# A causal-attention kernel with a channel mix behind it: the second batch's first pair of heads loaded ahead of the key weights, and the whole order of work written anew

## The chip, the cores and the metric

The kernel runs on one NeuronCore of a Trainium2 chip, as one program. The metric is the device time of one execution in microseconds (us), the median over runs. Engines are named as in the profile: PE is TensorE's matmuls and PEld its weight loads, DVE is VectorE, ACT is ScalarE, POOL is GpSimd and SP is SyncE. The DMA engines, 16 of them, move data for all.

## The reference

Inputs q, k and v have 8 batches of 8 heads, 576 rows and 64 columns, in float32. The first part is attention in which a row sees the blocks of 64 rows up to its own. Its output, with the heads side by side, is x of 8 x 576 x 512. The second part mixes each row with the one before it and sends it through three weight matrices.

```python
scores = scale * np.matmul(q, k.transpose(0, 1, 3, 2))
mask = block_i >= block_j            # blocks of 64 rows
attn = softmax(np.where(mask, scores, -1e9))
x = np.matmul(attn, v)               # heads side by side: B, S, 512
xk = mu_k * x + (1.0 - mu_k) * x_prev
xr = mu_r * x + (1.0 - mu_r) * x_prev
k = np.maximum(xk @ w_k, 0.0)
out = sigmoid(xr @ w_r) * (k * k @ w_v)
```

## The kernel before

The work is cut into 678 tasks. A task is one step of one engine, for example one load, one group of matmuls that fills a PSUM buffer, or one exponential. Each call of `add` (L67) makes one, and the functions below make them batch by batch. The order in which the tasks are written into the program is not that in which they are made: the table `ORDER` (L15) lists the tasks' numbers, each with a count of filler matmuls behind a plus sign, and `PLACE` (L53) names the engine of each task that may stand on several (P for POOL, D for DVE, A for ACT). `Plan.order` (L95) reads both. Each engine then does its own tasks strictly in that order, and waits where a task's inputs or its buffer are not ready. Buffers come from rings: four of PSUM (`ps`), four for q and k (`nb`), two each for their transposed forms (`qkt`), v as loaded (`lv`) and v in half precision (`vo`), ten for exponentials (`e`).

For each batch b the tasks are these, with the names that the text uses.

- Loads. `add_qk` (L235) loads k and q in pairs of heads on POOL's DMA queue (L249) and turns them on DVE (L260). For the first two batches (`HALVES`) a task loads two heads' rows with two DMAs, and the scores of a pair need only that pair. `add_v` (L272) loads v from SP (L284) and casts it (L207 to L216). `add_w` (L310) loads the key weights WK (four DMAs), the gate weights WR (two) and the value weights WV (four), all on POOL's queue (L324), after the first batch's q and k.
- Scores. `add_unit` (L349) multiplies k by q (L365) in small matmuls of 32 by 64 tiles, six units per batch, and takes the exponential on ACT (L386). For the first two batches a unit is cut into two halves of 8 to 24 matmuls, one per pair of heads. Later batches have units of 16 or 32 matmuls.
- Sums and products. `add_part` (L506, first batch, in two parts) and `add_av` (L426, the others) multiply the exponentials by a column picker for the sums (L524, L449) and by v (L544, L460: tasks T, A and B). DVE inverts the sums (L405 to L421) and normalises (L556, L489, L497) into `xt`.
- Mix. `add_mix` (L572) makes xk and xr of each quarter of the columns: a difference or two scalings on POOL, DVE or ACT (L580, L584), and two multiplications on DVE (L600, L604).
- Channel mix, for every 512 rows of all batches: `add_pk` (L623) is the key product (L644), its relu on ACT or DVE (L659, L661) and the square (L669, L671). `add_pr` (L677) is the gate product (L687) and a tanh (L697). `add_pv` (L703) is the value product (L721), the last multiplication on DVE (L731), and the store from SP (L740).

A first task, `spare` (L749), does 27 filler matmuls (L222) whose output nobody reads, until the first q and k are there. The other fillers stand ahead of sums and products: 1, 1 and 9 in the first batch.

Of the kernel before, what the change touches and what calls it, by code (L numbers as in the profile page):

```python
# [12 lines left out]
ALU = mybir.AluOpType  # L13

ORDER = """  # L15
# [35 lines left out]
"""  # L51

PLACE = (  # L53
    "DDDDPDPAPADDAPPAADAADPPDDPAPDPAAPPDADAPPPDAADAPDDAPDPDPDPAADPAAAADPAAA"
    "AAAAADPDADPAADPAPAPAPDDDAADAADPDAAPAAAPADAPADAADPADAA")


class Plan:
# [8 lines left out]
    def add(self, key, alts, fn, deps=(), uses=(), **info):  # L67
        t = {"key": key, "alts": alts, "eng": alts[0], "fn": fn,
             "deps": [d for d in deps if d is not None],
             "uses": list(uses), "fill": 0, "info": info}  # L70
        for b in t["uses"]:
            b["left"] += 1
        self.tasks.append(t)
        return t
# [37 lines left out]
def kernel(  # L112
# [12 lines left out]
    nc = tc.nc  # L125
    B, H, S, D = q.shape
    C = H * D
    DF = moe_w_k.shape[1]
    P = 128
# [3 lines left out]
    GH = 4  # L133
    QC = P // GH
    JT = S // D
    RW = 32
    TOK = S // RW
# [21 lines left out]
    LW = TOK * D  # L159
# [13 lines left out]
    def new(buf):  # L173

        return slots[buf["ring"], buf["slot"]]

    identb = consts.tile([P, P], BF)
# [21 lines left out]
    HALVES = (0, 1)  # L199
    add = plan.add  # L200
# [17 lines left out]
    def unread(t, dst):  # L218


        for _ in range(t["fill"]):
            nc.tensor.matmul(  # L222
                dst, identb,
                identb[:, :].unsqueeze(1).to_broadcast([P, 4, P]),
                start=True, stop=True)
# [9 lines left out]
    def add_qk(b, g, n):  # L235

        src, qkt = (q, k)[n], qkt_buf[b]
        nb = plan.buf("nb")  # L240

        def rows():
            return new(nb)

        def fetch(eng, me):
            parts = ([(D * y, D, GH * y + 2 * g, 2) for y in range(2)]
                     if b in HALVES else [(0, P, GH * g, GH)])
            for p0, np_, h0, nh in parts:
                nc.gpsimd.dma_start(  # L249
                    rows()[p0:p0 + np_],  # L250
                    src[b, h0:h0 + nh].rearrange(
                        "y (r j) d -> (y r) (j d)", j=TOK))
        t = add(f"qkld {b} {g} {n}", ("POOL",), fetch, uses=[nb], kind="ldc",
                kb=P * LW * 4 / 1024, starts=2 if b in HALVES else 1)

        if n:
            loads.setdefault(b, (nb, t))

        def turn(eng, me):
            nc.vector.transpose(  # L260
                new(qkt)[:, n, g].rearrange("p t e -> p (t e)").bitcast(
                    FP).rearrange("p (r j) -> p j r", r=RW),
                rows()[:, :].bitcast(FP).rearrange(
                    "p (j s) -> p j s", s=RW))
        evac["qkt", b, g, n] = add(f"turn {b} {g} {n}", ("DVE",), turn, [t],
                                   uses=[nb, qkt], kind="turn", cols=S)
# [436 lines left out]
    def add_pv(c, j0):  # L703
# [42 lines left out]

    wbuf = plan.buf("ps")

    add("spare", ("PE",), lambda eng, me: unread(me, new(wbuf)[:, 0]), uses=[wbuf],  # L749
        kind="spare", cols=[])  # L750
    mu_ready = []

# [81 lines left out]
```

## Time and profile before

| what | value |
|---|---|
| median of 3 runs | 260.37 us (259.85, 260.37, 262.7) |
| profiled execution | 262.33 us, of which the span from first to last instruction is 260.2 |
| mean granted TensorE clock | 0.980 |
| PE busy | 242.6 us, 93% of the span, 4058 matmuls |
| DVE, ACT, POOL busy | 188.8, 162.4 and 80.3 us |
| share of the chain that ended last | PE 84%, DMA 6%, ACT 3%, "issue" 3% |

Times in the profile count from the span's start. A busy PE is not PE at its peak, since a matmul's end is modelled. In the chain of work that ended last, a row gives a start, a duration and what ran or was waited for; the number behind an x is a count of instructions. "Issue" is time in which an engine waits for nothing that the program's own instructions tell. A row of busy time by stretches has, for each engine, the busy microseconds and the count of instructions that started, then the granted clock, the DMA engines' busy share and the GB/s that they moved. Idle time matters only on the engine that sets the end.

### The profile page before, as it was taken

The page shows a single profiled execution, that of the slowest core. Times are in us where ns is not written, and L with a number is a line of the kernel's source. Part 1 is how long each engine was busy: PE and PEld are TensorE (multiplying, and loading weights), DVE is VectorE, ACT ScalarE, POOL GpSimd, SP SyncE. Part 2 cuts the span into 40 slices and gives each one's busy share as a digit, 9 for nine tenths or more (in the row PEclk, how much of TensorE's full clock was granted, in tenths as well). Part 3 has the DMA queues.
Part 4 walks back from the last instruction along what each step waited for, and adds up shares of the span by engine and source line. Part 5 has one row for each costly group of instructions (what it writes and reads, how often), then busy time and mean ns, then how long its engine had stood idle before and what let it go on. Part 6 is the DMA issues. An engine that isn't in the chain of part 4 may idle for free.

```text
span 260.2 us, 8926 instructions
## 1 busy us (share of the span) xinstructions
PE 242.6 (93%) x4058; PEld 132.3 (51%) x4058; DVE 188.8 (73%) x233; ACT 162.4 (62%) x184; POOL 80.3 (31%) x88
## 2 busy tenths in 40 slices
PE   8859498879999999999999999999999999999994
PEld 3536356654454446644454487444554764444442
DVE  1737889597888699899688969884699389444322
ACT  1456048877656969796777786786887743274220
POOL 6074256841405610060455234420000221142000
PEclk9988989997999999999999999999999999999999
DMA  5999996899699995449785930021002200300224
GB/s 88 194 165 189 207 217 103 134 191 215 102 253 238 168 208 181 90 96 215 196 137 97 215 110 3 3 98 65 4 5 81 83 5 12 150 3 0 81 82 161
DMA packets 49189, 31.50 MB, mean 121 GB/s; under 512 B 38528, under 2 KB 39808, under 8 KB 49152
## 3 DMA queue, kind: packets, MB, share of 16 engines
q1 hardware_dynamic: 40128, 18.29, 29.7%
q0 software_dynamic: 6688, 12.06, 27.6%
q10 hardware_dynamic: 2336, 0.59, 1.5%
q8 instruction: 31, 0.51, 0.8%
q14 instruction: 6, 0.05, 0.1%
HBM read 33.56 MB, written 9.44 MB: 165 GB/s over the span
## 4 chain that ended last, share of the span: by engine, by line
PE 84%; DMA 6%; ACT 3%; issue 3%; DVE 1%; POOL 0%; ACTq 0%; DVEq 0%; POOLq 0%
PE t_ps L644 25%; PE t_ps L721 23%; PE t_ps L687 12%; PE t_ps L365 10%; PE t_ps L460 8%; PE t_ps L449 4%; DMA t_lv<-in_v_dram 4%; ACT t_e L386 2%; PE t_ps L544 2%; DMA t_nb<-in_k_dram 1%; DMA out_dram<-t_o 1%; PE t_ps L222 1%; DVE t_o L731 1%; PE t_ps L524 1%; ACT L293 0%
## 5 line engine op out<-in xcount | busy, mean ns | idle before, releaser
L386 ACT ACTIVATE t_e<-t_ps 128x1024 f16<-128x1024 f32 (+4 forms) x98 | 87.6, 957 | 30.9 <-PE t_ps L365 30.1
L644 PE MATMUL t_ps<-t_xk,WK 128*128 128x512 f16 (+3 forms) x416 | 66.9, 314 | 0.4 <-ACT t_e L386 0.3
L721 PE MATMUL t_ps<-WV,t_k 128*128 128x512 f16 (+1 forms) x296 | 64.6, 374 | 0.0
L671 POOL TENSOR_TENSOR t_k<-t_kr 128x1024 f16<-128x1024 f32 x16 | 30.5, 1907 | 76.9 <-DVE t_kr L661 62.5
L644 PEld LDWEIGHTS <-WK 128*128 128x128 f16 x416 | 37.0, 98 | 26.1 <-issue 2.4
L721 PEld LDWEIGHTS <-t_k 128*128 128x128 f16 x296 | 28.1, 98 | 33.1 <-issue 1.9
L365 PE MATMUL t_ps<-t_qkt 32*64 32x64 bf16 (+7 forms) x1344 | 37.3, 290 | 6.1 <-ACT t_e L386 3.8
L260 DVE STREAM_TRANSPOSE t_qkt<-t_nb 128x576 f32<-128x576 f32 x32 | 38.1, 1242 | 1.5 <-PE t_ps L365 1.0
L697 ACT ACTIVATE t_t<-t_ps 128x1024 f32<-128x1024 f32 x18 | 18.5, 1028 | 31.5 <-PE t_ps L687 31.5
L687 PE MATMUL t_ps<-WR,t_xr 128*128 128x512 f16 x144 | 35.1, 390 | 0.4 <-ACT t_e L386 0.4
L659 ACT ACTIVATE t_kr<-t_ps 128x1024 f32<-128x1024 f32 x22 | 22.4, 1024 | 18.8 <-PE t_ps L644 18.3
L365 PEld LDWEIGHTS <-t_qkt 32*64 32x64 bf16 x1344 | 21.8, 106 | 22.9 <-issue 17.9
L731 DVE SCALAR_TENSOR_TENSOR t_o<-t_t,t_ps 128x1024 f32<-128x1024 f32 (+2 forms) x20 | 22.1, 1108 | 14.9 <-PE t_ps L721 9.9
L661 DVE TENSOR_SCALAR t_kr<-t_ps 128x1024 f32<-128x1024 f32 x14 | 17.1, 1224 | 19.5 <-PE t_ps L644 19.4
L584 POOL TENSOR_TENSOR t_d<-t_xt 128x576 f32<-128x576 f32 (+2 forms) x10 | 11.6, 1162 | 36.3 <-DVE t_xk L604 13.5
L687 PEld LDWEIGHTS <-t_xr 128*128 128x128 f16 x144 | 13.7, 100 | 17.2 <-issue 2.5
L460 PE MATMUL t_ps<-t_e,t_vo 64*32 64x512 f16 (+7 forms) x1120 | 21.6, 295 | 0.0
L460 PEld LDWEIGHTS <-t_vo 64*32 64x32 f16 x1120 | 14.9, 95 | 8.8 <-issue 4.5
L604 DVE SCALAR_TENSOR_TENSOR t_xk<-t_d,MU,t_xt 128x576 f16<-128x576 f32 (+2 forms) x24 | 19.2, 802 | 0.1
L497 DVE TENSOR_TENSOR t_xt<-t_ps,t_rt 128x1024 f32<-128x1024 f32 x14 | 16.9, 1218 | 3.2 <-PE t_ps L460 3.1
L580 ACT ACTIVATE t_d<-t_xt,MU 128x576 f32<-128x576 f32 (+1 forms) x24 | 16.8, 751 | 3.7 <-DVE t_xr L604 2.6
L214 POOL CAST t_vo<-t_lv 128x1152 f16<-128x1152 f32 x8 | 9.7, 1216 | 30.5 <-PE t_ps L460 19.3
(40 smaller groups left out, 181.7 us busy)
## 6 DMA issues: line engine op xcount, KB each, us to landing
out_dram<-t_o SPq DMA_DIRECT2D x17, 512.0 KB, 3.3
t_lv<-in_v_dram SPq DMA_DIRECT2D x30, 288.0 KB, 6.3
t_nb<-in_k_dram POOLq DMA_DIRECT2D x12, 288.0 KB, 6.4
t_nb<-in_q_dram POOLq DMA_DIRECT2D x12, 288.0 KB, 6.2
t_nb<-in_k_dram POOLq DMA_DIRECT2D x8, 144.0 KB, 6.3
t_nb<-in_q_dram POOLq DMA_DIRECT2D x8, 144.0 KB, 6.3
WK<-in_moe_w_k_dram POOLq DMA_DIRECT2D x4, 256.0 KB, 6.7
WV<-in_moe_w_v_dram POOLq DMA_DIRECT2D x4, 256.0 KB, 9.0
```

Source lines behind the costliest of these rows:

```text
L260: nc.vector.transpose(new(qkt)[:, n, g].rearrange("p t e -> p (t e)").bitcast(FP).rearrange("p (r j) -> p j r", r=RW), rows()[:, :].bitcas ...
L365: nc.tensor.matmul(new(ms[a // 2])[y * D:y * D + D, a % 2, col:col + n], qkt[rows, 1, g, t * D:t * D + D, f], qkt[rows, 0, g, q0:q0 + n, f ...
L386: nc.scalar.activation(new(e)[:, 2 * h:2 * h + 2, 0:w], new(ms[h])[:, :, 0:w], AF.Exp, scale=ISQ)
L460: nc.tensor.matmul(PA[o, u, HALF + f * D:HALF + f * D + D] if kind == "T" else PA[o, u, lo - D:lo - D + n], weight(b, u, c, t % JT, f), E[ ...
L604: e.scalar_tensor_tensor(dst, dt[:, 0, 0:W], MU1[:, n, cc % 2, cc // 2:cc // 2 + 1], x, ALU.mult, ALU.add)
L644: nc.tensor.matmul(ps[:, x, y * w + a:y * w + a + n], WK[:, cc, jc * P:(jc + 1) * P], MIX[0][:, cc, at:at + n], start=(cc == 0), stop=(cc ...
L659: nc.scalar.activation(kt, ps, AF.Relu, scale=ROOT)
L671: (nc.vector if eng == "DVE" else nc.gpsimd).tensor_tensor(dst, KR, KR, ALU.mult)
L687: nc.tensor.matmul(ps[:, x], MIX[1][:, cc, g:g + P], WR[:, cc], start=(cc == 0), stop=(cc == CCn - 1))
L697: nc.scalar.activation(new(tb), new(m), AF.Tanh, scale=0.5)
L721: nc.tensor.matmul(ps[:, x, cols], k2[:, jc, at:at + P], WV[:, jc, cols], start=(jc == 0), stop=(jc == JCn - 1))
L731: nc.vector.scalar_tensor_tensor(new(o)[:, xs, cols], new(tb)[:, xs, cols], 1.0, new(m)[:, xs, cols], ALU.add, ALU.mult)
```

## The change

The two tables are written anew. Most of the 678 tasks stand in another place of the order, 71 of them on another engine; the last 21 stand as before. The two places below are those that the prediction speaks of. Numbers of buffers are part of the names: t_nb_107 to 110 are the four q and k buffers, t_ps_142 to 145 the four PSUM buffers, and t_e_115 to 124 the exponentials.

POOL, right behind the first batch's first value cast (a piece of the difference, - before, + now; the loads of 64 x 1152 are pairs of heads of the second batch):

```order
 L214 CAST t_vo_113<-t_lv_105 128x1152
-L324 DMA WK<-in_moe_w_k_dram 128x1024 x4
-L324 DMA WR<-in_moe_w_r_dram 128x1024 x2
 L249 DMA t_nb_107<-in_k_dram 64x1152 x2
-L584 ISA
-L584 TENSOR_TENSOR t_d_131<-t_xt_125 128x256
+L214 CAST t_vo_113<-t_lv_106 128x1152
 L249 DMA t_nb_108<-in_q_dram 64x1152 x2
+L328 DMA WK<-in_moe_w_k_dram 128x1024 x4
 L249 DMA t_nb_109<-in_k_dram 64x1152 x2
+L588 ISA
+L588 TENSOR_TENSOR t_d_131<-t_xt_125 128x256
```

The second batch's first k and q come ahead of WK, with a value cast between them that stood on DVE; the second pair follows WK, and WR, no longer in this piece, comes behind that pair.

ACT, from the end of the first batch's exponentials. Before (t_e_122 to 124 are the first three exponentials of the second batch; t_t_138 is the first gate product's tanh):

```order
L697 ACTIVATE t_t_138<-t_ps_143 128x1024
L580 ACTIVATE t_d_130<-t_xt_125,MU_157 128x320 x2
L386 ACTIVATE t_e_122<-t_ps_145 128x1024
L386 ACTIVATE t_e_123<-t_ps_144 128x1024
L386 ACTIVATE t_e_124<-t_ps_143 128x1024
L386 ACTIVATE t_e_115<-t_ps_145 128x1024
L386 ACTIVATE t_e_116<-t_ps_142 128x1024
L386 ACTIVATE t_e_117<-t_ps_143 128x2x320
```

And now (t_kr_132 and 133 are the relus of the first two key products, on DVE before):

```order
L390 ACTIVATE t_e_122<-t_ps_144 128x1024
L390 ACTIVATE t_e_123<-t_ps_142 128x1024
L390 ACTIVATE t_e_124<-t_ps_143 128x1024
L390 ACTIVATE t_e_115<-t_ps_144 128x1024
L390 ACTIVATE t_e_116<-t_ps_142 128x1024
L663 ACTIVATE t_kr_132<-t_ps_145 128x1024
L390 ACTIVATE t_e_122<-t_ps_143 128x1024
L663 ACTIVATE t_kr_133<-t_ps_144 128x1024
L390 ACTIVATE t_e_123<-t_ps_142 128x1024
L390 ACTIVATE t_e_124<-t_ps_145 128x1024
L701 ACTIVATE t_t_138<-t_ps_143 128x1024
```

The first five exponentials of the second batch now stand ahead of the first tanh, and the key products' relus stand among those of the second pair. PE's order is the same one: each exponential reads the PSUM buffer of the score step ahead of it, so five half score steps now come ahead of the first key product, and the gate product, which was the first step behind the first batch, comes after two key products and three more half steps.

The rest of the diff: the load of the first two batches is written with one loop over the halves and a source of three dimensions, with the same two DMAs; `spare` does its filler in two calls of 10 and 17 with an empty loop between them. The filler ahead of the first batch's second sums goes from 9 to 10, and the two single ones are gone.

```diff
 ORDER = """
-1 0+27 5 3 9 2 7 11 6 15 12 16 13 17 4 29 33 56 30 10 60 34 64 57 68 8 61 72
+1 5 0+27 3 9 7 2 11 15 12 6 16 13 17 4 29 33 56 30 10 60 34 64 57 68 8 61 72
...
 PLACE = (
-    "DDDDPDPAPADDAPPAADAADPPDDPAPDPAAPPDADAPPPDAADAPDDAPDPDPDPAADPAAAADPAAA"
+    "PADAPPDPDPPPDAAAPPPAAPPDPAAPDDDAPAPPDPDPPPDPAAADADAADADAADDADAAAPAAAPA"
...
         def fetch(eng, me):
-            parts = ([(D * y, D, GH * y + 2 * g, 2) for y in range(2)]
-                     if b in HALVES else [(0, P, GH * g, GH)])
-            for p0, np_, h0, nh in parts:
+            if b in HALVES:
+                for y in range(2):
+                    a = GH * y + 2 * g
+                    nc.gpsimd.dma_start(
+                        new(nb)[y * D:y * D + D, :],
+                        src[b, a:a + 2].rearrange(
+                            "h (r j) d -> h r (j d)", j=TOK))
+            else:
                 nc.gpsimd.dma_start(
-                    rows()[p0:p0 + np_],
-                    src[b, h0:h0 + nh].rearrange(
+                    rows(), src[b, GH * g:GH * g + GH].rearrange(
                         "y (r j) d -> (y r) (j d)", j=TOK))
...
-    add("spare", ("PE",), lambda eng, me: unread(me, new(wbuf)[:, 0]), uses=[wbuf],
+    SHORT = 0
+
+    def spare(eng, me):
+        dst, rest = new(wbuf)[:, 0], me["fill"]
+        me["fill"] = min(rest, 10)
+        unread(me, dst)
+        for n in range(SHORT):
+            at = n % GH * RW
+            nc.tensor.matmul(dst[at:at + RW, 0:D], identb[:, 0:RW],
+                             identb[:, 0:D], start=True, stop=True)
+        me["fill"] = max(rest - 10, 0)
+        unread(me, dst)
+    add("spare", ("PE",), spare, uses=[wbuf],
         kind="spare", cols=[])
```

More of the change, by code (lines that the diff above doesn't have):

```diff
@@ L15 @@
 ORDER = """
[35 rows of a table removed]
[35 rows of a table added]
 """
 PLACE = (
-    "DDDDPDPAPADDAPPAADAADPPDDPAPDPAAPPDADAPPPDAADAPDDAPDPDPDPAADPAAAADPAAA"
-    "AAAAADPDADPAADPAPAPAPDDDAADAADPDAAPAAAPADAPADAADPADAA")
+    "PADAPPDPDPPPDAAAPPPAAPPDPAAPDDDAPAPPDPDPPPDPAAADADAADADAADDADAAAPAAAPA"
+    "PAAAAAPADADAADDDPAAAPDPDPDAAAAADDAPAAADAPADDDAADPAADP")
 class Plan:
@@ L245, in fetch @@
         def fetch(eng, me):
-            parts = ([(D * y, D, GH * y + 2 * g, 2) for y in range(2)]
-                     if b in HALVES else [(0, P, GH * g, GH)])
-            for p0, np_, h0, nh in parts:
+            if b in HALVES:
[6 more added lines that the diff above has]
+            else:
                 nc.gpsimd.dma_start(
-                    rows()[p0:p0 + np_],
-                    src[b, h0:h0 + nh].rearrange(
+                    rows(), src[b, GH * g:GH * g + GH].rearrange(
                         "y (r j) d -> (y r) (j d)", j=TOK))
         t = add(f"qkld {b} {g} {n}", ("POOL",), fetch, uses=[nb], kind="ldc",
-                kb=P * LW * 4 / 1024, starts=2 if b in HALVES else 1)
+                kb=P * LW * 4 / 1024, starts=1 + (b in HALVES))
         if n:
```

68 rows, old and new, of the table ORDER are left out of this document.

## The prediction

> **What bounds the kernel now.** I read the page's slices first, then the chain that ended last in order of time, then busy time by stretches laid along what the chain showed. Slices are 6.5 us; the rows are TensorE's busy tenths, its granted clock and the DMA engines' share.
>
> ```profile
> PE   8859498879999999999999999999999999999994
> PEclk9988989997999999999999999999999999999999
> DMA  5999996899699995449785930021002200300224
> ```
>
> From the tenth slice (58.5 us) on TensorE is full until the last products. All loss that another order can win back lies in the first nine slices, where the DMA engines are full as well. The clock dips there three times. The chain names what TensorE waited for (start us, us, what):
>
> ```profile
> 16.94 0.77 DVE t_vo L214
> ...
> 18.23 0.41 issue
> ...
> 25.03 0.09 issue
> ...
> 27.52 3.79 issue
> 31.31 1.21 PE t_ps L544 x41
> 32.52 3.13 PE t_ps L687 x8
> 35.65 1.75 PE t_ps L644 x16
> 37.40 1.51 PE t_ps L365 x26
> ...
> 47.02 1.89 PE t_ps L687 x8
> ...
> 50.65 0.21 PE t_ps L460 x13
> 50.86 1.36 PE t_ps L449 x60
> ...
> 52.81 1.85 PE t_ps L644 x16
> 54.66 1.32 PE t_ps L460 x72
> ...
> 58.36 0.81 issue
> ...
> 62.74 3.56 PE t_ps L721 x16
> ...
> 66.31 0.59 PE t_ps L365 x31
> ...
> 73.81 1.40 PE t_ps L460 x79
> ```
>
> "Issue" is a wait for nothing that the program names, 3.79 us of it at one place. The gaps end at 18.64, 25.12, 31.31 and 59.17. Busy time between those ends (count of matmuls and of weight loads in brackets) and in the stretch ahead of them, and, in a fence of its own, in a later one with idle DMA engines:
>
> ```profile
> 11.10:18.63 7.53, 4.35 (x143) 2.77 (x132) 2.88 (x5) 5.69 (x9) 4.30 (x7) 0.96 1.12 167
> 18.63:25.11 6.48, 6.39 (x128) 3.81 (x128) 5.58 (x12) 4.16 (x5) 2.90 (x6) 0.78 1.14 197
> 25.11:31.30 6.19, 2.40 (x128) 1.87 (x128) 5.00 (x11) 0.00 (x0) 2.30 (x5) 1.00 1.13 206
> ...
> 53.40:59.16 5.76, 3.83 (x129) 2.53 (x127) 5.69 (x8) 4.86 (x6) 1.66 (x3) 0.99 1.19 193
> ```
>
> ```profile
> 155.45:159.19 3.74, 3.74 (x128) 2.64 (x133) 3.74 (x5) 2.65 (x4) 3.73 (x3) 1.00 0.02 4
> ```
>
> ```profile
> q8 instruction: 31, 0.51, 0.8%
> ```
>
> The stalls are 256 TensorE instructions apart (128 matmuls, 128 weight loads), and one queue (packets, MB, share) fetches instructions in 31 packets. So TensorE's program arrives in blocks of 256, and I call the place where one ends a border. With DMA engines at 1.13 to 1.19 a block takes 5.76 to 6.48 us to cross, however little work is in it: the one from 25.11 holds 2.40 us. With DMA engines at 0.02 a block of 3.74 us passes without idle time.
>
> On this point the Trainium skill ("Runtime: NRT & Kernel Launch", section "Instruction fetch mechanics") agrees with the count, blocks of 256 instructions, and says that crossing one is mostly hidden; the 3.79 us row contradicts the second half wherever the DMA engines are full.
>
> The second loss is the clock. These stretches are laid along its dips:
>
> ```profile
> 11.23:14.65 3.42, 2.34 (x80) 1.78 (x72) 1.23 (x1) 3.42 (x5) 0.32 (x1) 1.00 1.38 204
> 14.65:18.06 3.41, 1.68 (x61) 0.90 (x53) 1.12 (x2) 2.14 (x4) 3.41 (x6) 1.00 0.86 129
> 18.06:21.47 3.41, 3.02 (x100) 2.23 (x81) 2.97 (x7) 1.05 (x2) 1.88 (x4) 0.50 1.18 199
> ...
> 28.30:31.71 3.41, 0.40 (x25) 0.39 (x32) 3.41 (x7) 0.00 (x0) 0.52 (x1) 1.00 1.13 207
> 31.71:35.12 3.41, 3.41 (x62) 1.62 (x41) 2.87 (x5) 0.00 (x0) 1.45 (x3) 0.50 1.16 224
> ...
> 55.61:59.02 3.41, 1.61 (x85) 0.96 (x70) 3.38 (x5) 2.51 (x4) 0.09 (x1) 1.00 1.21 201
> 59.02:62.43 3.41, 3.26 (x91) 1.83 (x98) 2.08 (x4) 2.33 (x3) 0.00 (x0) 0.50 1.13 207
> ```
>
> A stretch of 3.41 us at half clock follows each one in which TensorE was busy 1.68, 0.40 or 1.61 us, and none follows 2.34. The limit lies between 1.68 and 2.34, so idle time of 1.07 to 1.73 us in one such stretch halves the next. A halved stretch full of work costs 1.7 us.
>
> **The change, part by part.** *Loads.* When the loads are issued now (start us, duration, engine):
>
> ```profile
> 15.42 2.40 POOL L324 DMA_DIRECT2D WK<-in_moe_w_k_dram  x4
> ...
> 18.85 1.09 POOL L249 DMA_DIRECT2D t_nb<-in_k_dram  x2
> ...
> 24.25 1.08 POOL L249 DMA_DIRECT2D t_nb<-in_q_dram  x2
> ```
>
> The k rows of the pair move from 18.85 to about 15.5. The q rows move from 24.25 to about 18: ahead of them POOL makes the second value cast, which VectorE made from 16.94 on, when its load had landed. The key weights follow at about 19, the second pair of heads at about 21, the gate weights last. Every transfer is still there, so the DMA engines stay full to about the same time. No step that needs the later transfers is near: the key weights, issued some 4 us later than before, are first used at about 36. Cost and gain of the loads themselves: nothing, down to the border at 31.31. Up to there both orders hold the same TensorE work between the borders, scores and products of the first batch, and the borders set its end. (The filler goes from 9 to 10 matmuls and loses two single ones, inside that wait. The two calls in `spare` still make 27 filler matmuls, and `fetch` the same two transfers: nothing.)
>
> *The block from 31.31.* Before, it holds the rest of a product, gate and key products (pr, pk) and three score steps: in chain rows 1.21 + 3.13 + 1.75 + 1.51, and TensorE is still behind when the next block could be there. Now it holds the same rest of 61 small matmuls and then five half score steps of the second batch, 64 matmuls, before the first key product. That is 125 of 128: only three matmuls of the key product fit. Five half steps at 1.51/3 = 0.50 us are 2.5, about 3.4 with the clock halved to 35.12, and the exponentials pace them: by about 36.4 TensorE is at the border. Crossing takes 6.2 to 6.5 from 31.31, bounds 5.8 and 7.5 (the block between 11.10 and 18.63 took 7.53): 37.7, a new wait of 1.3 us.
>
> *From there to the first value product* (L721, at 62.74 before; the same set of steps precedes it in both orders). Rest of the key product, 13 of 16 matmuls: 1.5. Seven half scores at 0.50: 3.5. Three key products at 1.85: 5.55. Two gate products at 1.89: 3.78. Four scores of the third batch at 0.59: 2.36. The second batch's sums and products: 1.36 + 1.32 + 0.21 + 1.40 = 4.29. One wait for an exponential, by the differences of start times: 0.25. Sum 21.2; 37.7 + 21.2 = 58.9. The exponentials no longer come in one run behind the scores but mixed with key and gate products, so TensorE's waits for them go.
>
> *The border at the third score of the third batch.* The block ahead of it holds 1.89 + 1.32 + 0.21 + 0.59 = 4.0 us. It needs at most 3.74 with idle DMA engines and 5.76 to 6.48 with full ones: a wait of 0 to 2.5. The value weights' and third batch's loads are asked for a few us earlier now and run out about then; I take 1.0, which is under the 1.07 that halves the clock. So 59.9.
>
> *Behind it.* The first key product of the next 512 rows stands right behind two value products now, where before three score and product steps stood between. By these rows VectorE must first do a normalisation (1.22), six multiplications and a difference of that size (7 x 0.80) and a transpose (1.24), 8.1 us, or 9.3 with the transpose that stands ahead of them; TensorE has 2 x 3.56 + 2 x 0.59 = 8.3 of other work: a wait of 0 to 1.0, I take 0.3.
>
> ```profile
> L260 DVE STREAM_TRANSPOSE t_qkt<-t_nb 128x576 f32<-128x576 f32 x32 | 38.1, 1242 | 1.5 <-PE t_ps L365 1.0
> ...
> L604 DVE SCALAR_TENSOR_TENSOR t_xk<-t_d,MU,t_xt 128x576 f16<-128x576 f32 (+2 forms) x24 | 19.2, 802 | 0.1
> L497 DVE TENSOR_TENSOR t_xt<-t_ps,t_rt 128x1024 f32<-128x1024 f32 x14 | 16.9, 1218 | 3.2 <-PE t_ps L460 3.1
> ```
>
> From there on TensorE is full in both and its work is the same. **Sum:** 62.74 - 59.9 - 0.3 = 2.5 us off the profiled execution, whose span is 260.2 in a time of 262.33. Of these, about 1.5 are the halved stretch at 59.02, and the profiled execution is 2 us over the median 260.37, near the highest run (262.7): the median run may not have that stretch. I give half of it back: 2.5 - 0.75 = 1.75, which makes 258.6.
>
> **The rivals.** *The two new borders cost nothing.* The waits of 1.3 and 1.0 go: 258.6 - 2.3 = 256.3. For it: crossing is free where the DMA engines idle. Against: the same transfers fill them to about 60 us, and three blocks in a row took over 6 us. The Trainium skill's sentence on hidden crossings, above, would give this time.
>
> *The clock is halved behind the border at 37.7.* The stretch around it has 1.3 us idle, inside the 1.07 to 1.73 in which the rows leave it open; price 1.7, so 260.3 and no difference. The Trainium skill ("TensorE: Matmul & The Clock Gate", section "What's actually happening") lets the clock fall only after a whole idle window of about 3.4 us, by which this can't happen; the rows show it after stretches that were nearly half busy, so it stays a rival.
>
> *Slower: the later border halves the clock too.* If the transfers still run at 53 to 57 us, the block with 4.0 us of work takes 6.3, a wait of 2.3 in place of 1.0, and that is past 1.73: the next stretch is halved, 1.7. With the halving at 37.7: 258.6 + 1.3 + 1.7 + 1.7 = 263.3; with the later alone 261.6; together about 262.4. It decides from a wait of 1.1 to 1.7 us there. For it: the block at 53.40 did just this before. Against: fewer transfers are left by then.
>
> *The pair's early arrival changes nothing* because its scores stand behind 31.31 in the program: then only the order behind counts. The sum has it so already: it is inside the forecast, at the same 258.6.
>
> **How the numbers follow.** Forecast 0.50 (258.6, its own range 257.2 to 260.0), hidden fetch 0.15 (256.3), clock halved once 0.20 (260.3), later border 0.15 (262.4). 1% is 2.6 us, about what can be told from no change. Faster by over that, under 257.8: 0.15 and a quarter of the forecast, 0.28. Slower, over 263.0: half the last rival, 0.08. Within: 0.64. The range from 256.4 to 261.6 leaves out about half the first and most of the last rival, 0.2 in all.
>
> **What would show it.** Right: gaps called issue still end near 18.6, 25.1 and 31.3, each 128 matmuls apart; a new one ends at 37 to 38 in the first key product, and the first value product starts at 59 to 61. The exponentials of the second batch start at 33 to 34. Wrong: no gap at 37 to 38; a half-clock stretch from about 38.5; the first value product after 62; or new idle time on TensorE after 70 us, which would make the loss one of the later order, on which nothing here rests.

## The result, and the profile after

| what | before | after |
|---|---|---|
| median of 22 runs each, one chip | 260.86 us (259.65 to 263.1) | 258.72 us (257.2 to 260.64) |
| ratio of after to before | | 0.9904, 95% interval 0.9879 to 0.9929 |
| profiled execution, and its span | 262.33, 260.2 | 260.4, 258.6 |
| mean granted clock of that execution | 0.980 | 0.978 |

The change makes the kernel about 1% faster: by the interval 1.9 to 3.2 us. Medians count every run, while ratios, here and below, leave out the slow ones (two of after's, of 401 and 479 us, which the range above leaves out too, and a few that lie over 1.5% above the fastest of their kernel), and a ratio is not the quotient of the two medians.

A part of the gain lies outside the span from first to last instruction: time less span is 2.1 to 2.2 us in nearly all runs with the order of before, and 1.7 to 1.9 in all with the new one. Why these 0.3 to 0.4 us go was not looked into.

The page of after, the same three rows of slices, then its chain in order of time (start us, us, what; "issue" is a wait that the program does not name), with the rows that answer to those of before:

```profile
PE   8777499968999999999999999999999999999994
PEclk9999779997999999999999999999999999999999
DMA  6999999978794799299466920070003100400224
```

```profile
53.90 1.52 PE t_ps L464 x86
...
56.01 2.94 issue
58.95 0.22 PE t_ps L369 x2
59.17 2.01 PE t_ps L464 x72
...
62.19 4.00 PE t_ps L725 x16
66.19 0.59 PE t_ps L369 x31
66.78 3.56 PE t_ps L725 x16
70.34 3.45 PE t_ps L648 x16
```

The first value product (L725, L721 before) starts at 62.19, only 0.55 earlier than before's 62.74. Ahead of it stands a wait of 2.94 us at the third score of the third batch, and a stretch at half clock behind it adds to its price. Busy time between the borders, and along the clock's dips (first PE, then PEld, DVE, ACT, POOL; then the granted clock, the DMA share, GB/s):

```profile
23.99:30.19 6.20, 2.41 (x133) 1.89 (x133) 5.29 (x12) 0.00 (x0) 3.43 (x6) 0.90 1.13 204
30.19:36.38 6.19, 6.14 (x129) 3.65 (x129) 4.73 (x7) 3.63 (x5) 1.77 (x3) 0.55 1.14 215
...
51.67:58.96 7.29, 4.35 (x130) 2.35 (x129) 6.33 (x8) 3.93 (x4) 1.78 (x3) 1.00 0.71 118
28.93:32.34 3.41, 2.17 (x70) 1.52 (x73) 1.81 (x5) 0.00 (x0) 1.69 (x4) 0.50 1.14 216
32.34:35.76 3.42, 3.42 (x60) 1.93 (x52) 3.42 (x5) 3.01 (x4) 1.24 (x2) 0.50 1.13 211
56.24:59.65 3.41, 0.70 (x26) 0.47 (x33) 1.96 (x2) 1.37 (x2) 2.47 (x4) 1.00 0.09 10
59.65:63.07 3.42, 3.42 (x99) 1.93 (x79) 1.81 (x2) 1.41 (x2) 0.82 (x2) 0.50 1.03 178
25.52:28.93 3.41, 0.86 (x66) 0.54 (x51) 3.33 (x9) 0.00 (x0) 2.27 (x4) 1.00 1.14 208
```

The borders stand at the steps where the prediction put them, 128 matmuls apart (17.52, 23.99, 30.19, 36.38, 44.74, 51.67, 58.96), the first three some 1.1 us sooner than in before. The block from 30.19 is full of work, because the clock was at half in two stretches in a row, so the new wait at its end nearly vanishes into the slow work. The wait that ends at 58.96 leaves 0.70 us of work in its stretch, and the next one runs at half clock: it is the mechanism of the last rival, in this execution.

One execution is not the median, though. The same kernel was profiled once more in the last experiment (f_after), in an execution of 258.09 us with a span of 256.3:

```profile
36.54 0.13 issue
...
55.95 0.78 issue
56.73 0.22 PE t_ps L369 x2
56.95 1.32 PE t_ps L464 x72
58.27 0.59 PE t_ps L369 x31
58.86 3.56 PE t_ps L725 x16
```

```profile
30.20:36.67 6.47, 5.23 (x128) 3.10 (x128) 5.07 (x8) 4.69 (x5) 2.06 (x4) 0.74 1.14 214
51.48:56.73 5.25, 4.37 (x142) 2.32 (x127) 5.18 (x8) 4.04 (x5) 0.00 (x0) 1.00 1.08 180
36.67:58.86 22.19, 20.89 (x491) 14.07 (x491) 21.65 (x25) 17.66 (x19) 9.29 (x13) 1.00 1.03 168
```

Here TensorE stands still for 1.24 of the 6.47 us ahead of the border at 36.67 (the chain puts all but 0.13 of that down to a load of k, but the matmul that goes on there needs the third piece of WK, which had landed at 29.1, and in f_hold below the same matmul starts at 36.08, before that load's first packets land at 36.5), the border at the third score costs 0.78, no half clock follows, and the first value product starts at 58.86. The two executions of one program are 3.33 us apart at the first value product, and that one wait and the slow work behind it are nearly all of it: (2.94 - 0.78) + (2.01 + 1.01 - 1.32 - 0.59) = 2.16 + 1.11 = 3.27.

For the gain, busy time from the third border to the first value product in before, in this execution and in the profiled one above:

```profile
31.31:62.74 31.43, 27.84 (x620) 18.14 (x620) 25.72 (x31) 22.03 (x25) 16.08 (x19) 0.89 0.99 169
```

```profile
30.20:58.86 28.66, 26.12 (x619) 17.18 (x619) 26.72 (x32) 22.35 (x24) 11.36 (x17) 0.94 1.05 178
```

```profile
30.19:62.19 32.00, 28.48 (x619) 18.28 (x619) 26.91 (x31) 22.45 (x24) 12.69 (x18) 0.87 1.02 176
```

Of the 2.77 us between the first two rows, 1.72 are busy time that a halved clock had stretched (two stretches in before, one in this execution) and 1.05 are idle time. Of before's 3.6 us idle, 2.8 are waits for exponentials; of this execution's 2.5 some 2 are waits at borders. So one kind of wait was traded for a smaller one of another kind. The third row shows all of this given back, and 0.6 us more.

The profiled execution of before, 262.33 us, is 1.5 us over the median, though. An execution with the order of before that lies near it is that of e2 below (260.84 us; only the pair stands elsewhere, which pays nothing):

```profile
31.59:61.47 29.88, 26.43 (x619) 17.90 (x619) 25.43 (x31) 22.07 (x26) 16.00 (x19) 0.95 0.98 161
```

It has 3.45 us idle, 3.1 of them waits for exponentials, and one halved stretch like f_after's. The 2.75 us between this execution and that of 258.09 us are 1.39 up to the third border (31.59 against 30.20), 1.22 from there to the first value product (29.88 against 28.66), 0.2 lost behind it, and 0.35 outside the span. So near the medians the first part, ahead of the third border, is the largest.

### The profile page after: what moved, and what is told of

Read it like the earlier page. It is cut to its first block, busy times and chain, and to the rows that moved or that the text cites. A ratio compares the mean times of both kernels' runs of the same rounds, so it can differ in the third digit from the quotient of the medians.

```text
span 258.6 us, 8913 instructions
## 1 busy us (share of the span) xinstructions
PE 242.0 (94%) x4057; PEld 131.9 (51%) x4057; DVE 189.5 (73%) x230; ACT 163.6 (63%) x186; POOL 78.1 (30%) x89
## 4 chain that ended last, share of the span: by engine, by line
PE 78%; DMA 9%; ACT 5%; POOL 2%; issue 2%; DVE 2%; DVEq 0%; POOLq 0%; ACTq 0%
PE t_ps L648 25%; PE t_ps L725 23%; PE t_ps L691 11%; PE t_ps L464 8%; PE t_ps L369 8%; DMA t_nb<-in_k_dram 4%; PE t_ps L453 4%; DMA t_lv<-in_v_dram 3%; ACT t_e L390 3%; DMA t_nb<-in_q_dram 3%; POOL t_nb L249 1%; DVE t_xr L608 1%; DVE t_xk L608 1%; ACT L297 0%; DVE t_qkt L264 0%
## 5 line engine op out<-in xcount | busy, mean ns | idle before, releaser
L648 PE MATMUL t_ps<-t_xk,WK 128*128 128x512 f16 (+3 forms) x416 | 66.6, 314 | 0.5 <-ACT t_e L390 0.4
L725 PE MATMUL t_ps<-WV,t_k 128*128 128x512 f16 (+1 forms) x296 | 65.2, 376 | 0.1
L648 PEld LDWEIGHTS <-WK 128*128 128x128 f16 x416 | 36.8, 98 | 25.5 <-issue 2.1
L675 POOL TENSOR_TENSOR t_k<-t_kr 128x1024 f16<-128x1024 f32 x12 | 22.7, 1892 | 78.5 <-ACT t_kr L663 53.0
L725 PEld LDWEIGHTS <-t_k 128*128 128x128 f16 x296 | 28.1, 98 | 32.7 <-issue 1.7
L369 PE MATMUL t_ps<-t_qkt 32*64 32x64 bf16 (+7 forms) x1344 | 38.4, 295 | 5.9 <-issue 3.2
L264 DVE STREAM_TRANSPOSE t_qkt<-t_nb 128x576 f32<-128x576 f32 x32 | 37.5, 1243 | 8.7 <-PE t_ps L369 5.0
L663 ACT ACTIVATE t_kr<-t_ps 128x1024 f32<-128x1024 f32 x26 | 26.6, 1024 | 19.4 <-PE t_ps L648 19.2
L691 PE MATMUL t_ps<-WR,t_xr 128*128 128x512 f16 x144 | 34.0, 380 | 0.3 <-ACT t_e L390 0.3
L588 POOL TENSOR_TENSOR t_d<-t_xt 128x576 f32<-128x576 f32 (+2 forms) x12 | 14.4, 1200 | 41.9 <-DVE t_xt L501 21.2
L464 PE MATMUL t_ps<-t_e,t_vo 64*32 64x512 f16 (+7 forms) x1120 | 20.9, 291 | 0.0
L665 DVE TENSOR_SCALAR t_kr<-t_ps 128x1024 f32<-128x1024 f32 x10 | 12.2, 1222 | 11.7 <-PE t_ps L648 11.6
L608 DVE SCALAR_TENSOR_TENSOR t_xr<-t_d,MU,t_xt 128x576 f16<-128x576 f32 (+2 forms) x24 | 20.1, 849 | 0.1
```

The source lines that it names most:

```text
L264: nc.vector.transpose(new(qkt)[:, n, g].rearrange("p t e -> p (t e)").bitcast(FP).rearrange("p (r j) -> p j r", r=RW), rows()[:, :].bitcas ...
L369: nc.tensor.matmul(new(ms[a // 2])[y * D:y * D + D, a % 2, col:col + n], qkt[rows, 1, g, t * D:t * D + D, f], qkt[rows, 0, g, q0:q0 + n, f ...
L464: nc.tensor.matmul(PA[o, u, HALF + f * D:HALF + f * D + D] if kind == "T" else PA[o, u, lo - D:lo - D + n], weight(b, u, c, t % JT, f), E[ ...
L608: e.scalar_tensor_tensor(dst, dt[:, 0, 0:W], MU1[:, n, cc % 2, cc // 2:cc // 2 + 1], x, ALU.mult, ALU.add)
L648: nc.tensor.matmul(ps[:, x, y * w + a:y * w + a + n], WK[:, cc, jc * P:(jc + 1) * P], MIX[0][:, cc, at:at + n], start=(cc == 0), stop=(cc ...
L663: nc.scalar.activation(kt, ps, AF.Relu, scale=ROOT)
```

## The experiments

*Theory A*: TensorE's program comes in blocks of 256 instructions over the DMA engines, and while these are full the borders decide; the change gains by the work that stands between borders. *Theory B*: the pair's early arrival pays, since its scores no longer wait. Two more theories came up on the way: *C*, that a gain lay in the chip of one run, and *D*, that the order of the exponentials and not the fetch sets the time to 59 us. Each batch of runs (e1 to e4, e5 to e12, and the last four) shares the runs of before on its own chip (29, 17 and 17 runs); each kernel has one profiled execution.

| kernel | median us (lowest to highest, runs) | before there | ratio, 95% interval |
|---|---|---|---|
| e1_pair_back | 259.35 (257.13 to 260.48, 12) | 261.88 | 0.994, 0.9903 to 0.9977 |
| e2_pair_alone | 261.06 (260.24 to 262.57, 12) | 261.88 | 1.0012, 0.9977 to 1.0048 |
| e3_late_v | 256.22 (255.65 to 257.3, 6) | 261.88 | 0.9845, 0.9799 to 0.989 |
| e4_shift | 260.17 (257.13 to 262.03, 12) | 261.88 | 0.9953, 0.991 to 0.9996 |
| e5_late_v12 | 257.58 (256.52 to 259.55, 6) | 261.22 | 0.9856, 0.9813 to 0.99 |
| e8_no_filler | 257.88 (255.38 to 260.41, 6) | 261.22 | 0.9845, 0.9798 to 0.9893 |
| e9_before_late_v | 261.05 (258.96 to 262.26, 12) | 261.22 | 0.9983, 0.9953 to 1.0013 |
| e12_key_first | 256.21 (254.88 to 257.03, 6) | 261.22 | 0.9787, 0.9749 to 0.9824 |
| f_after (the changed kernel) | 258.26 (257.05 to 259.66, 6) | 261.48 | 0.989, 0.9851 to 0.9928 |
| f_hold (as e3) | 256.63 (255.69 to 257.05, 6) | 261.48 | 0.983, 0.9795 to 0.9865 |
| f_key | 259.19 (256.67 to 261.59, 12) | 261.48 | 0.9908, 0.9874 to 0.9942 |
| f_both (as e12) | 257.07 (256.01 to 258.28, 6) | 261.48 | 0.9846, 0.9808 to 0.9883 |

**The pair put back behind the key weights, all else as changed (e1).** POOL's rows, - changed kernel, + this one; the pair's two turns on DVE stand later accordingly:

```diff
-DMA t_nb_107<-in_k_dram 64x1152 x2
+DMA WK<-in_moe_w_k_dram 128x1024 x2
 CAST t_vo_113<-t_lv_106 128x1152
+DMA WK<-in_moe_w_k_dram 128x1024 x2
+DMA t_nb_107<-in_k_dram 64x1152 x2
 DMA t_nb_108<-in_q_dram 64x1152 x2
-DMA WK<-in_moe_w_k_dram 128x1024 x4
```

> The changed kernel with one part undone: the second batch's first pair of k and q is issued behind the key weights again (and its two transposes stand later on VectorE, so that they don't hold it up); all else is the new order. Theory A (TensorE's program arrives in blocks of 256 instructions, each border takes some 6.2 us while the DMA engines are full, and the order of work behind the border near 30 us is what pays): the pair still lands before about 29 us and its scores stand behind the border at 30 to 31, so 258.7 to 259.9 against 258.7 of the changed kernel, at most 1.2 slower. Theory B (the pair's early arrival is what pays): the gain goes, 260.5 to 261.5.

Over half of the gain stays, 0.994 against 0.9904 and 0.989 for the changed kernel on other chips; the intervals overlap, so it isn't shown that the pair's place costs anything here. The time lies in the range of Theory A. Its chain has the same waits in the same places, some 0.8 us later than the 30.19 and 0.55 to 0.84 later than the 36.38 and 36.67 of the changed kernel (rows out of the chain, start us and us):

```profile
23.63 1.20 issue
...
36.17 1.05 issue
...
56.50 1.61 issue
```

**The pair put ahead in the kernel before, nothing else (e2).** POOL's rows, - before, + this one:

```diff
 CAST t_vo_113<-t_lv_105 128x1152
+DMA t_nb_107<-in_k_dram 64x1152 x2
+DMA t_nb_108<-in_q_dram 64x1152 x2
 DMA WK<-in_moe_w_k_dram 128x1024 x4
 DMA WR<-in_moe_w_r_dram 128x1024 x2
-DMA t_nb_107<-in_k_dram 64x1152 x2
 ISA
 TENSOR_TENSOR t_d_131<-t_xt_125 128x256
-DMA t_nb_108<-in_q_dram 64x1152 x2
```

> The kernel before with one part alone: the second batch's first pair of k and q is issued ahead of the key and gate weights, all else stays. Theory A: the same as before, 260.4 to 261.3, since nothing that uses the pair stands earlier. Theory B: faster by over 1 us, under 259.8.

No difference, 1.0012 with 1 inside the interval. Theory B falls: what the title of the change names pays nothing by itself. The chain ahead of its first value product is of interest for a later experiment:

```profile
56.98 1.25 DVE t_qkt L258
58.22 1.06 DVE t_xt L495
...
59.48 1.95 ACT t_e L384 x2
61.43 0.04 issue
61.47 3.61 PE t_ps L719 x16
```

**The borders moved (e4).** The first filler is cut from 27 matmuls to 23 and `SHORT` set to 32, so 28 more matmuls stand ahead of everything and every border falls 28 matmuls earlier in the program.

```diff
-1 5 0+27 3 9 7 2
+1 5 0+23 3 9 7 2
...
-    SHORT = 0
+    SHORT = 32
```

> The changed kernel with its first filler made of 23 long matmuls and 32 tiny ones in place of 27 long ones: 28 matmuls (56 instructions) more ahead of everything, in a stretch where TensorE waits for the first loads anyway. Theory A: the gaps called issue near 30, 36 and 59 us end at about the same times but 28 matmuls earlier in the program: the first where the last product of the first batch begins or just ahead of it, the second in the half scores, the third ahead of the last 28 matmuls before its place now. 259.0 to 260.6, since less work is done when each border ends. Rival (the gaps belong to the tasks in which they stand): same tasks, 258.4 to 259.0.

The waits moved by just that: its chain has them inside other steps than the changed kernel's. L526 are the first batch's sums, L546 its products, L367 scores:

```profile
16.60 1.80 issue
18.40 0.35 PE t_ps L526 x7
...
28.38 1.31 issue
29.69 1.25 PE t_ps L546 x72
...
33.17 2.99 issue
36.16 1.59 PE t_ps L367 x19
```

Counted from the first matmul, these waits stand ahead of the 480th and the 608th in the changed kernel and here alike, and that at the third score ahead of the 992nd in both (58.96 and 59.24 us). A wait that follows the count of instructions, and neither the data nor the step, is the border's. By the ratio (0.9953) the kernel loses about half of the gain, but the interval overlaps those of the changed kernel on other chips; that where a border falls is worth some time is likely, not shown, nor which border cost what, since all moved.

**One value load held (e3).** The third batch's second half of v (two DMAs), asked for at 48.0 and 48.6 us, is held until behind the second tanh by a copy of one column into its buffer on ACT (it is asked for at 55.0 and 55.7 in e3's trace); - changed kernel, + this one:

```diff
 ACTIVATE t_t_139<-t_ps_145 128x1024
+COPY t_lv_106<-MUS 128x1
 ACTIVATE t_e_120<-t_ps_143 128x1024
...
+    for b, m in [(2, 1)]:
+        add(f"late {b} {m}", ("ACT",), lambda eng, me, ld=lds[b, m]:
+            nc.scalar.copy(new(ld)[:, 0:1], MUS[:, 0, 0:1]),
+            uses=[lds[b, m]], kind="hold")
```

> The changed kernel, but the second half of the third batch's v load is held back (by a copy of one column on ScalarE behind the second gate tanh, near 55 us), so that it does not run while TensorE's block at 52 to 59 us is fetched. Theory A: that gap called issue, 2.94 us in the changed kernel's profile, shrinks to 0.3 to 1.7 and the half-clock stretch behind it goes in most executions: 256.0 to 257.7. Rival (the gap is not set by the transfers that run beside it): the gap stays at 2.5 to 3.2 and the time at 258.4 to 259.0.

It is 1.55% under before. The wait at the third score, of which 0.3 to 1.7 us were expected to stay, is gone, and so is the half clock behind it; the block ahead of that border now takes 4.28 us with the DMA engines half idle:

```profile
51.50:55.78 4.28, 4.18 (x144) 2.29 (x129) 4.21 (x7) 3.46 (x5) 0.00 (x0) 1.00 0.49 83
```

**The second batch's loads of v held as well (e5).** From about 15 us to the end of the first batch's exponentials; - as e3, + this one:

```diff
 ACTIVATE t_e_121<-t_ps_144 128x2x320
+COPY t_lv_105<-MUS 128x1
+COPY t_lv_106<-MUS 128x1
```

> The kernel with the late third-batch v load, and the second batch's v loads held back too, from about 15 us to about 23 us (two one-column copies on ScalarE behind the first batch's last exponential). If TensorE's blocks wait for the small packets of the v loads, the blocks up to 30 us are fetched faster, the border near 30 us comes 0.5 to 2 us earlier, and the time is 254.3 to 255.8. If they wait just as long beside POOL's transfers alone, that border stays at 30 to 31 and the time at 255.8 to 256.8.

The third border came at 29.92 instead of 30.22, and the median of 257.58 us lies above both ranges: 0.9856 against 0.9845, so nothing is gained. In the trace the held loads are asked for from 24.4 on and run beside the block that ends at 29.92. So the run shows that this hold pays nothing, and leaves open which transfers the early borders wait for.

**The filler ahead of the second sums taken out (e8).** As e3, with `76+10` written `76` in the order.

> The kernel with the late third-batch v load, without the 10 filler matmuls ahead of the first batch's second sums. Theory A (the border near 30 us sets the time, whatever the clock does ahead of it): the clock may fall to half for a stretch between 24 and 30 us, at no cost; each border stands 10 matmuls later in the program: 255.6 to 256.4 against 256.2. Rival (the filler pays, since it keeps the clock up): 257.2 to 259.

The ratio is that of e3, but its six runs spread over 5 us where those of e3 spread over 1.7, and their median of 257.88 lies in the rival's range. Whether the filler pays is not decided by these runs.

**The same hold in the kernel before (e9).** - before, + this one:

```diff
 ACTIVATE t_e_120<-t_ps_145 128x1024
+COPY t_lv_106<-MUS 128x1
 ACTIVATE t_e_121<-t_ps_142 128x1024
```

> The kernel before with the second half of the third batch's v load held back in the same way, behind ScalarE's exponential near 61 us. Theory A: the block that it fetches from 53 to 59 us (0.81 us of wait called issue, 1.13 just ahead of it, and a half-clock stretch behind) comes sooner; the first half of that v load still runs, so a part is won: 259.4 to 260.8 against 260.9 to 261.9 of the kernel before on the same chips, 0.4 to 1.8 less. If the changed order alone made the hold pay: no difference.

No difference: 0.9983, with 1 inside the interval. The standstill at the border fell from 1.00 to 0.36 us (from the start of the matmul ahead of it to that of the next), at 59.27, but the first value product still starts at 62.13. Its chain says why, and e2's above says the same: in the order of before a turn and a normalisation on DVE and two exponentials end at the first value product, 4.5 us in one run, and a border ahead of them is hidden.

```profile
57.63 1.25 DVE t_qkt L258
58.88 1.06 DVE t_xt L498
...
60.14 1.95 ACT t_e L387 x2
62.09 0.04 issue
62.13 3.61 PE t_ps L722 x16
```

So a shorter wait at this border pays nothing in the order of before. In the new order those exponentials are done before TensorE comes to the border. But this run is a weak test of the hold itself, which takes little away there: beside that block the DMA engines stay as full as before's 1.19, most of it POOL's transfers. And e2, which holds nothing, has no standstill at this border at all.

```profile
54.04:59.27 5.23, 3.93 (x131) 2.63 (x128) 5.16 (x8) 4.33 (x6) 1.76 (x3) 1.00 1.19 193
```

**The first key product ahead of two score steps, with the hold (e12).** ACT's rows, - as e3, + this one; on TensorE the key product (t_ps_144) stands ahead of the fourth and fifth half score step:

```diff
-ACTIVATE t_e_115<-t_ps_144 128x1024
-ACTIVATE t_e_116<-t_ps_142 128x1024
-ACTIVATE t_kr_132<-t_ps_145 128x1024
+ACTIVATE t_kr_132<-t_ps_144 128x1024
+ACTIVATE t_e_115<-t_ps_142 128x1024
+ACTIVATE t_e_116<-t_ps_145 128x1024
```

> The kernel with the late third-batch v load, and the first key product placed ahead of the fourth and fifth half score steps of the second batch. Theory A: the block from 30 to 37 us has the same 128 matmuls, but 16 of them are the key product's, 1.85 us, in place of 13 of the key product behind the border; TensorE waits at that border about 1 us less and has 1.0 us less to do behind it: 255.0 to 255.8 against 256.2. Rival (the order within a block does not matter, the exponentials pace it): 256.0 to 256.8.

It gave the lowest ratio, 0.9787, but on another chip than e3, and the intervals overlap. So the hold, the move, both and neither went to one chip.

**Hold and move, two by two (f_after, f_hold, f_key, f_both).** f_hold is e3 and f_both e12; f_key has e12's move alone.

> The changed kernel itself, beside three variants of it on one chip. Both theories: 1.5 to 3 us under the kernel before, and in most profiled executions a wait of 1 to 3 us that ends near 59 us, ahead of the third score of the third batch, with a half-clock stretch near it.

> The changed kernel with one value load of the third batch held back until the second tanh. Theory A (the transfers that run beside the fetch of the block at 59 us cost the wait there): 2 to 3.5 us under the changed kernel on this chip. Theory C (that gain lay in the chip of the earlier run): within 1 us of the changed kernel.

> The changed kernel with the first key product and its relu moved ahead of the fourth and fifth half score step, no load held. It moves work only in the blocks between 30 and 44 us. Theory A: PE is past the border near 36 us earlier by 0.5 to 1, but the border at the third score of the third batch is still set by its fetch, so most of that is lost again there: 0 to 1 us under the changed kernel, with a wait of 1.5 to 3.5 that ends at 57.5 to 59. Theory D (the exponentials' order, not the fetch, sets the time to 59 us): as fast as with the hold and the move together.

> The changed kernel with the hold and the move of the first key product together. Theory A: the move pays only when the later border is free: 2.5 to 4 us under the changed kernel, 0.3 to 1 under the one with the hold alone. Theory D: no better than the move alone.

The hold takes 1.63 us off the changed kernel (258.26 to 256.63): under the 2 us that Theory A expected at least, over the 1 us that Theory C allowed; the slowest run of f_hold is level with the fastest of f_after. With the move in both it takes 2.12 off (259.19 to 257.07). The move alone takes nothing off, and on top of the hold nothing either. Theories C and D fall, and so does the gain that I had read into e12. f_after itself missed its expectation of a wait of 1 to 3 us with a half-clock stretch: its one profile has 0.78 and no half clock behind it. f_key has the wait that Theory A gave it, 2.02 us (it ends at 56.77, sooner than expected), so the time won near 36 us was lost there; but that the move adds nothing behind the hold is a miss for the 0.3 to 1 us that A gave it.

How the hold does it is seen in the times at which the block ahead is asked for and comes. From the instruction queue's packets in the trace: the border crossed before it (the start of the first matmul behind it), the fetch's start and end, and when TensorE goes on at the third score, with the length of its standstill, from the start of the matmul ahead to that of the next (0.2 us more than the chain's wait).

```
kernel     crossed   fetch from   to      goes on   stood
after      51.67     56.14        57.37   58.96     3.1
f_after    51.48     53.66        54.96   56.73     1.0
e1         52.04     54.86        56.58   58.11     1.8
f_key      50.62     54.31        55.19   56.77     2.0
e3         51.50     52.92        53.89   55.78     under 0.2
f_hold     50.90     51.90        52.93   55.19     under 0.4
e12        50.57     51.43        52.85   54.71     under 0.2
f_both     51.01     52.29        53.25   55.14     under 0.2
e5         52.01     54.44        55.34   56.83     0.7
```

The fetch itself takes 0.9 to 1.7 us. What differs more is how long it waits to start: 2.2 to 4.5 us with the value load in flight, 0.9 to 1.4 with it held; e5, which holds it too but brings other loads later, has 2.4 and a ratio between the two. Where the DMA engines are idle, in before's stretch of 155.45:159.19, the fetch starts at 155.58, and the next one at 159.63, both within half a us of the border. The block's own row shows the same from the engines' side, f_hold against f_after's 51.48:56.73 above:

```profile
50.90:55.19 4.29, 4.19 (x144) 2.30 (x129) 4.22 (x7) 3.46 (x5) 0.00 (x0) 1.00 0.39 66
```

The version that beats both kernels is thus the change with one load held: 256.22 and 256.63 us in two batches, 1.5 to 1.7% under before.

## Why the prediction was right, step by step

The time (258.6 forecast, 258.72 measured) came out, and so did the mechanism: borders that follow the count of instructions, a new one in the first key product, and exponentials that TensorE no longer waits for. But that the number fits so well is in part luck: terms of the sum were off in opposite directions.

- *The loads themselves: nothing, up to the border at 31.31.* This was the step that failed. The third border came at 30.19 and 30.20 in two executions of the changed kernel, and at 28.83 to 30.46 in all others with its order and the pair ahead. It came at 31.03 with the pair put back (e1), and at 31.31, 31.59 and 32.41 in the three profiles with the order of before (before, e2, e9). So 1.1 us were won where I had put nothing. That e2 has the pair ahead and comes at 31.59 shows that the pair alone does not do it; why the new order's first blocks come sooner wasn't settled. The lead is there at the second border already (23.99 and 24.08 against 25.12).
- *A new wait of 1.3 us at a border in the first key product, at 37.7.* The place is right. Counted from the third border the block took 6.47 us in f_after, inside the forecast's 6.2 to 6.5, and TensorE stood still for 1.24 of them. It ended at 36.67 and not at 37.7 because of the 1.1 us above. In the profiled execution of after next to no wait was left (0.05 us in the row 30.19:36.38), because the clock was at half from 28.93 to 35.76 and TensorE came late to the border; the price was paid as slow work instead. One row behind this term was read wrongly: the block of 6.48 us was busy for 6.39 of them at a clock of 0.78, so slow work and not the border made it long.
- *21.2 us from there to the first value product, and a wait of 1.0 at the third score.* Together 22.2. In f_after it is 22.19, the row 36.67:58.86, with a wait of 0.78. In the profiled execution it is 62.19 - 36.38 = 25.8: 1.9 more of the wait, 1.1 of slow work behind it, and 0.5 at the border at 51.67. The bounds of 0 to 2.5 for that wait were too narrow at the top, and the 5.76 to 6.48 us for a block beside full DMA engines are not a floor: e2's 53.38:58.25 took 4.87 at a DMA share of 1.18, without a standstill. How long this wait is, and whether it halves the clock, differs from one execution to the next. The last rival had the mechanism right and the price about right, and was wrong for the median; by the prediction's own sign, a first value product after 62, that one execution counts for it. The rival of a half clock behind 37.7 came in neither execution.
- *A wait of 0.3 at the first key product of the next 512 rows.* It wasn't there: that product (70.34, L648) follows the value product at 66.78 without a gap.
- *"From there on TensorE is full in both and its work is the same."* Its work is, but it wasn't full: from the first value product to the end

```profile
62.74:102.74 40.00, 38.65 (x604) 19.95 (x602) 34.52 (x39) 29.56 (x34) 13.12 (x13) 1.00 0.99 200
102.74:260.20 157.46, 153.83 (x2363) 81.19 (x2360) 110.27 (x124) 98.52 (x109) 37.08 (x28) 1.00 0.33 82
```

```profile
62.19:102.19 40.00, 39.74 (x612) 19.69 (x612) 35.13 (x38) 32.13 (x38) 14.72 (x14) 0.99 0.91 176
102.19:258.60 156.41, 152.70 (x2364) 81.45 (x2348) 111.35 (x127) 95.18 (x104) 35.26 (x28) 1.00 0.34 87
```

  before's page had a wait of 0.71 for exponentials at 71.03, which the prediction does not count, and the new order has it no more: 197.46 us became 196.41, and of the first 40 us TensorE is busy 39.74 and no longer 38.65. In f_after the span is 256.3, so the same part takes 197.4 again: it met border waits of 0.87 and 0.39 there, which the profiled execution, 3.3 us later, did not. What TensorE gains it can lose at the next border.
- *Half of a halved stretch given back, 0.75.* Right in kind, too small: neither e2 nor e9 has before's half-clock stretch at 59 us, and they take 29.88 and 29.72 us from the third border to the first value product where before's profile took 31.43. So some 1.6 was to be given back.

The sums close: 1.1 + 2.8 + 0.0 = 3.9 us between the spans of before and f_after (260.2 and 256.3), and 1.1 - 0.6 + 1.05 = 1.6 between the two profiled ones. Against medians the forecast was a gain of 1.75, all of it behind the third border; the interval gives 1.9 to 3.2. Near the medians (e2 against f_after) 1.0 of the 2.75 us between them came from there, 1.39 from ahead of that border and 0.35 from outside the span, where the forecast has nothing. So what I gave too much to the part behind the border and nothing to the part ahead of it made up for each other in part. Of the rivals, "the new borders cost nothing" is refuted by e3 and f_hold: one wait at a border less is 1.6 us in the median. The rival that the pair's early arrival changes nothing is borne out by e2.

What stays open: why the same fetch waits 2.2 us in one execution and 4.5 in another, how much the pair ahead is worth in the new order (by e1's ratio about 1 us, the intervals overlap), why the first three borders come sooner there, and what the 0.35 us outside the span are.

## What to carry to other kernels

Where TensorE's waits lie a fixed count of instructions apart and the DMA engines are full, the program's own fetch is the late transfer. Look there for one load that nobody needs soon, and hold it: here that gave 1.6 us, while the pair of loads put first gave nothing by itself. Before you promise such a gain, look whether another chain ends at the same step and whether the hold empties the DMA engines at all, because in the order of before the same hold gave nothing. And compare executions near the medians: the two profiled ones of the changed kernel are 2.3 us apart.

## What the runs showed of the hardware

- TensorE goes on 1.2 to 1.8 us after the block's last packet, wherever it stood still for it: at f_after's six borders with a standstill of 0.7 us or more, 1.24 to 1.77 us lie between (16.54 to 17.81, 28.92 to 30.20, 35.43 to 36.67, 54.96 to 56.73, 76.97 to 78.26 and 83.64 to 85.01).
- The clock can stay at half through two stretches of 3.41 us: the one at 28.93 was busy for 2.17 us, already at half clock, and the next was halved as well. The prediction's limit of 1.68 to 2.34 lies above 2.17, if it is the same for a stretch at half clock. It is no sharp limit in busy time, though: f_key's stretch with 1.64 us busy has full clock behind it, and f_after's with 2.02 has half clock behind it (17.69 to 21.10).

```profile
54.99:58.40 3.41, 1.64 (x82) 1.20 (x89) 2.81 (x4) 2.05 (x2) 1.60 (x2) 1.00 0.39 79
```

```profile
14.27:17.68 3.41, 2.02 (x68) 1.58 (x68) 1.13 (x4) 3.41 (x6) 2.80 (x5) 1.00 0.83 129
```

- The mean granted clock doesn't tell which execution took less time: one of f_after's has 0.970 in 258.74 us, another 0.987 in 259.66.
